# Linear attention and a gated feed-forward layer: attention steps at new places, ten sums of h in another layer

## The chip, the cores and the metric

The kernel runs on one core of a Trainium2 chip. The metric is the device time of one execution in microseconds (us); for the kernel before, the median of 11 executions is given. The core has a matmul engine (PE), a vector engine (DVE), a scalar engine (ACT), a general engine (POOL), and a queue that here only sends transfers (SP). Each works through its own instructions in order and waits for the others by semaphores.

## The reference

```python
# q, k, v: (8 batches, 8 heads, 576 positions, 64); all float32
kv  = einsum('bhsd,bhse->bhde', k, v)
out = einsum('bhsd,bhde->bhse', q, kv)
out = out / sqrt(mean(out * out, axis=-1) + 1e-6) * g_norm
x   = out.transpose(0, 2, 1, 3).reshape(4608, 512)
gate = 1 / (1 + exp(-(x @ w_gate)))       # w_gate, w_val: (512, 1536)
return (gate * (x @ w_val)) @ w_out       # w_out: (1536, 512)
```

The feed-forward weights come as 64-bit floats and are converted on the chip.

## The kernel before

**Chunks.** The 4608 rows of x are cut into nine chunks c = 0 to 8 of 512 rows; a batch of attention has 576 rows. Chunk 0 is computed plainly, while the first two batches of attention run and the weights are converted. From c = 1 on the first layer (`first_layer_fast`), and from c = 2 on the second layer too (`second_layer_fast`), use a scheme of fast matrix multiplication: a 4 x 4 by 4 x 2 block product (the second layer: the same with its own order) is done in 26 products of sums of blocks in place of 32. `PRODUCTS1` and `PRODUCTS2` list, for each product, the letter of the PSUM region that it adds into, the two forms that it multiplies (a form is a raw block, 0 to 15, or a sum from `SUMS`), and the steps that follow it: `o5=A` is a copy by ACT, `o3=o3+D` an add by DVE, `s0` a sigmoid by ACT, and `o5*o1` a multiplication by POOL (in the last product of the last third, by DVE). There are five PSUM regions for these letters, so a letter's region is taken, added into again, and given back.

**First layer.** It has three thirds j = 0, 1, 2 of 26 products each; the product i of third j stands at place p = 26 j + i, so places run from 0 to 77. A product is two matmuls of 128x256 in float32, which the profile records as four. After each product the program issues, in this order: the product's own steps (`combine`), the attention steps that a table has for this place (`at`), one sum of h (two at i = 12 and 25), and POOL's transfers.

**Attention.** While chunk c is computed, batch c + 1 of attention runs between its products (c = 1 to 6). `feed(b)` returns its steps. `kv_mm` multiplies k and v of all heads (80 matmuls), and `kv_copies` takes the result out in four steps on ACT. The heads come in four pairs n0 to n0 + 3. A pair's q has a single buffer: `turn` transposes it on DVE in two steps (t0 to t3 are the steps of the four pairs), and after the second step SP is told to load the next pair's q. `two_pairs` then works on two pairs at once (u0, u1), in nine steps: u_mm (144 small matmuls), square (ACT), two sums (DVE), root (ACT), two norms (DVE), and two x turns. An x turn is two transposes on DVE and twelve or fewer transfers that put x into the chunk that it belongs to. The k and v of the next batch are loaded by `load_late` at the end of each second layer, twelve transfers on SP's queue, into the space of `h_more`.

**Sums of h.** The first layer's result h of a third is the input of the second layer, which needs 28 sums of its blocks per third (`SUMS`). The sums of third j are issued by POOL during third j + 1; those of the last third in the second layer, eight of them by DVE (`ON_VECTOR`) and twenty by POOL, two ahead of the first product and two after each finished product (`finish`).

**Sums of x and w.** The sums of the next chunk's x (`X_SUMS`, 18 on DVE) are issued in the second layer after the finished products that `at2` names. The sums of the first layer's weights (`w1_sums`) are made once, by POOL, in chunk 0, written to memory and loaded back in parts ("granules", four per third) for each chunk. The sums of the second layer's weights pass through a ring of ten buffers: ten loads (`load_w`) stand in the first layer and eight in the second, all on POOL's queue.

Of the kernel before, what the change touches and what calls it, by code (L numbers as in the profile page):

```python
# [20 lines left out]
def kernel(  # L21
# [13 lines left out]
    B, H, S, HD = q.shape  # L35
# [43 lines left out]
    first = first_ctx.__enter__()  # L79
# [274 lines left out]
    def feed(b):  # L354
# [94 lines left out]
        def turns_of(n):  # L449
# [3 lines left out]
        kv = [kv_mm] + [lambda i=i: kv_copies(i, range(3)) for i in range(2 * NC)]  # L453
        t0, t1, t2, t3 = (turns_of(n0 + i) for i in range(4))
        u0, u1 = two_pairs(n0), two_pairs(n0 + 2)
        return kv, list(zip(
            (3, 4, 19, 20, 28, 30, 31, 33, 34, 35, 36, 39, 41, 42, 45, 46, 48, 51, 53, 55, 56, 57, 61, 64, 71, 72),
            t0 + t1 + u0[:2] + t2[:1] + u0[2:3] + t2[1:] + u0[3:7] + t3 + u0[7:] + u1))

    def flush():  # L460
        while fill:
# [249 lines left out]
        s_ = h_at[v]  # L711
        return h_main[j][:, s_] if s_ < 4 * NT else h_more[:, j, s_ - 4 * NT]

    def h_sums(j):
        ops = []
        for v, (x, sign, y) in SUMS.items():
            eng = nc.vector if j == N3 - 1 and v in ON_VECTOR else nc.gpsimd
            ops.append((eng, lambda v=v, x=x, sign=sign, y=y, eng=eng: eng.tensor_tensor(  # L718
                out=h_form(v, j), in0=h_form(x, j), in1=h_form(y, j), op=op_of(sign))))
        return ops  # L720
# [12 lines left out]
    def w1_sums(j):  # L733
        for v in W_ORDER:
            x, sign, y = SUMS[v]
            nc.gpsimd.tensor_tensor(out=w1_slot(j, w_at[v]), in0=w1_slot(j, w_at[x]), in1=w1_slot(j, w_at[y]),  # L736
                                    op=op_of(sign))
# [43 lines left out]
    for f in range(4, NFT):  # L781
        if f == NFT - 1:
            last = at_ps()
            plain(0, f, (last[:, 0], last[:, 1]))
        else:
            plain(0, f, (mm_ps(), mm_ps()))
        if f == 8:
            second_batch[0][0]()
        elif f == 9:
            for step in second_batch[0][1:]:  # L790
                step()
        elif f == NFT - 1:
            w1_sums(0)
            w1_sums(1)

    ps = [mm_ps() for _ in range(G // P)]
# [106 lines left out]
    def first_layer_fast(c, at):  # L903
        for f in range(NFT):
            gv_tile(c, f)
        for j in range(N3):
            o = {f"t{n}": pair(temps[:, i]) for i, n in enumerate((0, 1, 8, 9))}
            for n in (3, 1, 2, 0):
                o[f"o{n}"] = pair(sg_tile())
            h = h_main[j].rearrange("p (g e t) c -> p g e (t c)", g=2, e=2)  # L910
            for n in range(4):
                o[f"o{4 + n}"] = h[:, :, n // 2, GH * (n % 2):GH * (n % 2) + GH]
            regions = {}
            for i, (name, hv, wv, steps) in enumerate(PRODUCTS1):
                part, p = next(n for n, r in enumerate(PARTS) if i in r), NPR * j + i
                new = name not in regions
                if new:
                    i_ = free.popleft()
                    regions[name] = i_, pair(bank(i_))
                ws = w1_form(c, j, part, hv)  # L920
                for g in range(2):
                    nc.tensor.matmul(regions[name][1][:, g], ws[:, g], xf[c][wv], start=(new and g == 0), stop=True,  # L922
                                     skip_group_check=True)
                combine(o, regions, steps, nc.vector if j == N3 - 1 and i == NPR - 1 else nc.gpsimd)
                give_all(regions, LAST1, i)
                for step in at.get(p, ()):
                    step()
                for _ in range(2 if i % HALF == HALF - 1 else 1):
                    if h_fill:
                        h_fill.popleft()[1]()  # L930
                if c > 1:
                    g_ = NPA * (N3 * (c - 2) + j) + part
                    if i == PARTS[part][-1] and p < NPR * N3 - 1:
                        load_granule(g_ + NPA)
                    k_, r = divmod(p - 30, 4)
                    if r == 0 and 0 <= k_ < NR:
                        load_w((c - 2) * NS + k_)
                elif p in (NPR, 2 * NPR):
                    keep_w1(j - 1)
                elif p == 2 * NPR + HALF:  # L940
                    for g_ in range(NPA):
                        load_granule(g_)
            if c > 1:
                h_fill.extend(h_sums(j))

    tok = [slice(P * i, P * i + P) for i in range(NT)]

# [63 lines left out]
    def second_layer_fast(c, at):  # L1011
        o = {f"t{n}": temps[:, i, 0:DH] for i, n in enumerate((0, 1, 8, 9))}
        rows = [sg_tile() for _ in range(NT)]
        for t in range(NT):
            for n in range(2):
                o[f"o{2 * t + n}"] = rows[t][:, DH * n:DH * n + DH]
        regions, used, done = {}, {}, count()
        dones = {18: 0, 22: 1, 24: 2, 25: 3}

        def product(i, js):  # L1020
            name, hv, wv, _ = PRODUCTS2[i]
            if i not in used:
                used[i] = name not in regions
                if used[i]:
                    regions[name] = take()
            ws = w_raw(wv) if wv < 8 else ring((c - 2) * NS + STREAM.index(wv))
            for j in js:
                nc.tensor.matmul(regions[name][1], h_form(hv, j), ws[:, j], start=(used[i] and j == 0),  # L1028
                                 stop=(j == N3 - 1), skip_group_check=True)

        def finish(i):
            _, _, wv, steps = PRODUCTS2[i]
            combine(o, regions, steps, nc.gpsimd)
            give_all(regions, LAST2, i)
            if wv > 7 and STREAM.index(wv) + NR < NS:
                load_w((c - 2) * NS + STREAM.index(wv) + NR)
            if i == 16:
                load_granule(NPA * N3 * (c - 1) + NPA - 1)
            if i in dones:
                t = dones[i]  # L1040
                if c == NG - 1 and t == NT - 1:
                    store(c, t, rows[t], slice(0, DH), (nc.sync, nc.scalar))
                else:
                    store(c, t, rows[t])
            elif c == NG - 1 and i == 23:
                store(c, NT - 1, rows[NT - 1], slice(DH, DM))
            for step in at.get(next(done), ()):
                step()
            sums_of_h(2)

        on_pool = deque(step for eng, step in h_fill if eng is nc.gpsimd)

        def sums_of_h(n):
            for _ in range(n):
                if on_pool:
                    on_pool.popleft()()

        sums_of_h(2)
        for eng, step in h_fill:
            if eng is nc.vector:  # L1060
                step()
        h_fill.clear()
        blocks, some = range(N3), range(N3 - 1)
        product(0, blocks)
        finish(0)
        for i in (1, 2, 6):
            product(i, some)
        product(3, blocks)
        finish(3)
        for i in range(1, NPR):  # L1070
            if i != 3:
                if i in (1, 2, 6):
                    if i == 6:
                        continue
                    product(i, (N3 - 1,))
                    finish(i)
                    if i == 2:
                        product(6, (N3 - 1,))
                        finish(6)
                else:  # L1080
                    product(i, blocks)
                    finish(i)
        load_late(c + 2)
# [11 lines left out]
    for c in range(1, NG):  # L1095
        at1, at2 = {}, {}
        if c + 1 < B:
            kv, first_ = second_batch if c == 1 else feed(c + 1)
            for p, step in first_ + ([(16 + p, step) for p, step in enumerate(kv)] if c > 1 else []):
                at1.setdefault(p, []).append(step)  # L1100
        if c + 1 < NG:
            p0, two = (23, 18) if c == 1 else (6, 0)
            p = p0
            for n, step in enumerate(lambda n=n, c=c: x_sum(c + 1, n) for n in range(len(X_SUMS))):
                at2.setdefault(p, []).append(step)
                p += (2 if c == 1 else 1) if n % 2 or n >= two else 0
        if c == 1:
            for n, step in enumerate(w_forms()):
                at2.setdefault(2 * n, []).append(step)
        first_layer_fast(c, at1)  # L1110
        if c == 1:
            sgs += [spare_sg] + more_sgs
        (second_layer_plain if c == 1 else second_layer_fast)(c, at2)
# [30 lines left out]
```

## Time and profile before

| What | us |
|---|---|
| median of 11 executions | 1050.69 |
| lowest and highest | 1046.60 and 1056.12 |
| the profiled execution | 1047.59 |
| its span in the profile | 1045.8 |
| PE busy | 1019.8 |
| DVE busy | 721.1 |
| POOL busy | 607.4 |
| ACT busy | 348.3 |

The profiled execution is one of the lower ones; its span leaves out 1.8 us around it. From the timeline of PE, the starts of the layers (us):

| c | first layer starts | lasts | second layer starts | lasts |
|---|---|---|---|---|
| 1 | 161.88 | 75.44 | 237.32 (plain) | 41.20 |
| 2 | 278.52 | 76.06 | 354.58 | 34.03 |
| 3 | 388.62 | 76.30 | 464.92 | 33.80 |
| 4 | 498.72 | 76.35 | 575.07 | 33.79 |
| 5 | 608.85 | 77.46 | 686.32 | 34.43 |
| 6 | 720.74 | 78.83 | 799.57 | 33.76 |
| 7 | 833.33 | 67.34 | 900.67 | 36.50 |
| 8 | 937.18 | 67.38 | 1004.56 | 41.25, with the end |

Lines of the profile are read so: in a list of waits, who waited for whom, then us in total, how often, and the longest. In a timeline: start, us, engine, line of the program, operation, out<-in, shape and count, and in brackets the idle time of the engine just before and what ended it. In the chain of waits: start, us, what. In a table of stretches: the stretch, its length, then the busy time and count of PE, PEld, DVE, ACT and POOL, the clock, the share of the DMA engines, and GB/s.

### The profile page before, as it was taken

What the parts mean: (1) busy time and instruction counts of PE and PEld (TensorE: products, weight loads), DVE (VectorE), ACT (ScalarE), POOL (GpSimd) and SP (SyncE); (2) the same over time, 40 slices, a digit from 0 to 9 for tenths busy, and PEclk for the clock granted to TensorE, in tenths of its full rate; (3) what the DMA queues carried; (4) which work ended last, traced back from release to release, by engine and by line L of the source; (5) the groups of instructions that cost most, each with busy time, mean ns of one, the idle gap of its engine ahead of it and who ended that gap; (6) DMA issues with size and microseconds to landing.
All of it is one profiled execution on the core that took longest, in us unless ns stands there. A gap on an engine that the chain in (4) does not pass through costs nothing.

```text
span 1045.8 us, 18194 instructions
## 1 busy us (share of the span) xinstructions
PE 1019.8 (98%) x6854; PEld 814.1 (78%) x6854; DVE 721.1 (69%) x1188; ACT 348.3 (33%) x604; POOL 607.4 (58%) x991
## 2 busy tenths in 40 slices
PE   9999999999999999999999999999999999999998
PEld 8544447784588888888888888788788888788876
DVE  4899898676557955776577756785488556755672
ACT  4653423440144204431444125411442033213320
POOL 0002999876148832985179507790488239923991
PEclk9999999999999999999999999999999999999999
DMA  9975301469768656865777576766576536653634
GB/s 265 262 250 178 119 27 52 154 222 354 253 183 252 215 168 217 259 219 167 226 232 244 173 208 198 228 194 177 172 253 210 164 109 231 209 159 113 233 112 116
DMA packets 98406, 203.31 MB, mean 194 GB/s; under 512 B 29840, under 2 KB 69008, under 8 KB 98320
## 3 DMA queue, kind: packets, MB, share of 16 engines
q0 software_dynamic: 28048, 138.43, 39.7%
q1 hardware_dynamic: 70016, 63.66, 21.8%
q8 instruction: 54, 0.88, 0.4%
q14 instruction: 32, 0.26, 0.1%
q10 hardware_dynamic: 256, 0.07, 0.0%
HBM read 168.30 MB, written 26.74 MB: 186 GB/s over the span
## 4 chain that ended last, share of the span: by engine, by line
PE 74%; POOL 12%; DVE 5%; DMA 4%; issue 2%; ACT 2%; SPq 0%; POOLq 0%; DVEq 0%; ACTq 0%
PE mm L922 32%; PE mm L1028 21%; PE mm L559 7%; PE mm L1001 4%; PE mm L799 4%; POOL h L718 4%; POOL h_more L718 3%; POOL h L885 3%; DMA q<-in_q_dram 3%; PE at L407 2%; DVE sg L893 1%; DVE h L893 1%; POOL w L967 1%; PE at L366 1%; DMA h_more<-in_v_dram 1%
## 5 line engine op out<-in xcount | busy, mean ns | idle before, releaser
L922 PE MATMUL mm<-xs,w 128*128 128x256 f32 x1428 | 335.0, 380 | 5.3 <-DVE sg L893 5.3
L922 PEld LDWEIGHTS mm<-xs,w 128*128 128x128 f32 x1428 | 269.5, 190 | 45.8 <-DVE sg L893 8.8
L922 PE MATMUL mm<-xT,w 128*128 128x256 f32 x948 | 231.4, 380 | 4.2 <-ACT temps L889 4.2
L922 PEld LDWEIGHTS mm<-xT,w 128*128 128x128 f32 x948 | 179.0, 190 | 32.3 <-ACT temps L889 5.3
L893 DVE TENSOR_TENSOR sg<-sg,mm 128x512 f32<-128x512 f32 (+1 forms) x169 | 99.0, 604 | 147.5 <-PE mm L922 100.5
L762 POOL DMA_DIRECT2D w<-kept x84 | 46.4, 552 | 228.1 <-PE mm L922 227.7
L1028 PE MATMUL mm<-w,h 128*128 128x256 f32 x558 | 127.2, 379 | 0.6 <-POOL h L885 0.5
L889 ACT COPY temps<-mm 128x512 f32<-128x512 f32 (+1 forms) x124 | 64.3, 540 | 182.7 <-PE mm L922 99.4
L885 POOL TENSOR_TENSOR h<-h,sg 128x512 f32<-128x512 f32 x72 | 93.8, 1321 | 46.8 <-ACT sg L882 26.8
L1028 PEld LDWEIGHTS mm<-w,h 128*128 128x128 f32 x558 | 105.9, 190 | 15.7 <-POOL h L885 1.4
L718 POOL TENSOR_TENSOR h<-h 128x128 f32<-128x128 f32 x189 | 99.1, 535 | 9.5 <-DVE h_more L718 6.4
L882 ACT ACTIVATE sg<-sg 128x512 f32<-128x512 f32 x96 | 59.0, 629 | 114.7 <-DVE sg L893 114.4
L1028 PE MATMUL mm<-w,h_more 128*128 128x256 f32 x390 | 90.4, 381 | 3.9 <-POOL h_more L718 3.8
L889 ACT COPY sg<-mm 128x512 f32<-128x512 f32 (+1 forms) x107 | 55.3, 516 | 93.3 <-PE mm L1028 47.4
L1028 PEld LDWEIGHTS mm<-w,h_more 128*128 128x128 f32 x390 | 73.4, 190 | 16.1 <-POOL h_more L718 5.0
L559 PE MATMUL mm<-xT,w 128*128 128x512 f32 x176 | 77.7, 594 | 0.0
L893 DVE TENSOR_TENSOR temps<-temps,mm 128x512 f32<-128x512 f32 (+1 forms) x93 | 58.1, 624 | 19.5 <-PE mm L1028 10.8
L736 POOL TENSOR_TENSOR h_more<-w 128x256 f32<-128x256 f32 x10 | 12.9, 1302 | 97.0 <-PE at L366 97.0
L889 ACT COPY h<-mm 128x512 f32<-128x512 f32 x48 | 28.1, 585 | 119.7 <-PE mm L922 119.7
L893 DVE TENSOR_TENSOR temps<-mm,temps 128x512 f32<-128x512 f32 (+1 forms) x62 | 39.0, 628 | 38.4 <-PE mm L922 16.3
L967 POOL DMA_DIRECT2D w<-kept x102 | 63.1, 619 | 2.4 <-issue 2.2
L559 PEld LDWEIGHTS mm<-xT,w 128*128 128x128 f32 x176 | 32.6, 190 | 37.0 <-issue 36.4
(144 smaller groups left out, 1414.1 us busy)
## 6 DMA issues: line engine op xcount, KB each, us to landing
w<-kept POOLq DMA_DIRECT2D x102, 384.0 KB, 4.2
w<-kept POOLq DMA_DIRECT2D x42, 896.0 KB, 5.9
w<-kept POOLq DMA_DIRECT2D x42, 768.0 KB, 5.8
w_ring<-kept POOLq DMA_DIRECT2D x24, 384.0 KB, 4.0
out_dram<-sg SPq DMA_DIRECT2D x110, 64.0 KB, 1.7
q<-in_q_dram SPq DMA_DIRECT2D x24, 288.0 KB, 6.4
st<-in_moe_w_gate_dram SPq DMA_DIRECT2D x12, 512.0 KB, 5.6
st<-in_moe_w_val_dram SPq DMA_DIRECT2D x12, 512.0 KB, 6.3
```

Of the source, the lines that this page charges most:

```text
L559: nc.tensor.matmul(self.ps[i], w[("wg", "wv")[i], self.f][:, m, :], xT[self.c][:, m, :], start=(m == 0), stop=(m == NMT - 1), skip_group_c ...
L718: ops.append((eng, lambda v=v, x=x, sign=sign, y=y, eng=eng: eng.tensor_tensor(out=h_form(v, j), in0=h_form(x, j), in1=h_form(y, j), op=op ...
L762: nc.gpsimd.dma_start(out=granule(g)[:, 0:n], in_=kept1[g // NPA % N3, g % NPA][:, 0:n])
L799: nc.tensor.matmul(ps[t], gv[0, f][:, P * t:P * t + P], w["wo", f], start=(f == 0), stop=(f == NFT - 1), skip_group_check=True)
L882: nc.scalar.activation(out=o["o" + step[1]], in_=o["o" + step[1]], func=AF.Sigmoid)
L885: mult.tensor_tensor(out=o[x], in0=o[x], in1=o[y], op=ALU.mult)
L889: nc.scalar.copy(out=o[out_], in_=o[expr])
L893: tt(out=o[out_], in0=o[x], in1=o[y], op=ALU.add if sign == "+" else ALU.subtract)
L922: nc.tensor.matmul(regions[name][1][:, g], ws[:, g], xf[c][wv], start=(new and g == 0), stop=True, skip_group_check=True)
L967: nc.gpsimd.dma_start(out=ring(i), in_=kept3[i % NS].rearrange("p (j n) -> p j n", j=N3))
L1001: nc.tensor.matmul(ps, gv[c, f][:, tok[t]], w2[:, f, :], start=(n == 0), stop=(n == NFT - 1), skip_group_check=True)
L1028: nc.tensor.matmul(regions[name][1], h_form(hv, j), ws[:, j], start=(used[i] and j == 0), stop=(j == N3 - 1), skip_group_check=True)
```

## The change

Four things are changed.

1. `feed` places its steps anew, and leaves the last two (the two x turns of u1) to the second layer: after finishes 4 and 5, or, in the plain second layer of c = 1, after matmuls 4 and 8. The steps of kv_mm and kv_copies go from places 16 to 20 to 17, 17, 19, 20 and 22. The sums of x in the second layer then begin after finish 12 in place of 6, the first eight of them two at a time (not in c = 1, nor where no attention is left).
2. Of the 28 sums of h of third j = 1, only 18 are issued in third j = 2; the ten others are issued in the second layer, behind the first 18 of j = 2 and ahead of that third's last ten.
3. The ten loads of the ring stand at places 20, 22, ... 38 in place of 30, 34, ... 66.
4. `w1_sums(0)` is issued after the plain block f = 10 in place of f = 15.

The places of the attention steps, c = 1 to 6:

| Step | before | after |
|---|---|---|
| turns of pair n0 | 3, 4 | 1, 5 |
| turns of n0 + 1 | 19, 20 | 14, 22 |
| u0: u_mm, square | 28, 30 | 27, 30 |
| turns of n0 + 2 | 31, 34 | 29, 31 |
| u0: sums, root | 33, 35, 36 | 32, 33, 37 |
| turns of n0 + 3 | 42, 45 | 38, 47 |
| u0: norms, x turns | 39, 41, 46, 48 | 46, 49, 52, 53 |
| u1: u_mm, square, sums, root | 51, 53, 55, 56, 57 | 53, 55, 56, 57, 60 |
| u1: norms | 61, 64 | 61, 63 |
| u1: x turns | 71, 72 | second layer, finishes 4 and 5 |

```diff
-        return kv, list(zip(
-            (3, 4, 19, 20, 28, 30, 31, 33, 34, 35, 36, 39, 41, 42, 45, 46, 48, 51, 53, 55, 56, 57, 61, 64, 71, 72),
-            t0 + t1 + u0[:2] + t2[:1] + u0[2:3] + t2[1:] + u0[3:7] + t3 + u0[7:] + u1))
+        first = list(zip((1, 5, 14, 22, 27, 29, 30, 31, 32, 33, 37, 38, 46, 47, 49, 52, 53, 53, 55, 56, 57, 60, 61, 63),
+                         t0 + t1 + u0[:1] + t2[:1] + u0[1:2] + t2[1:] + u0[2:5] + t3[:1] + u0[5:6] + t3[1:] + u0[6:] +
+                         u1[:7]))
+        return kv, first, u1[7:]
...
-    def h_sums(j):
+    SUMS_FIRST = 18
+
+    def h_sums(j, some):
         ops = []
-        for v, (x, sign, y) in SUMS.items():
+        for v, (x, sign, y) in list(SUMS.items())[some]:
...
+        elif f == 10:
+            w1_sums(0)
         elif f == NFT - 1:
-            w1_sums(0)
             w1_sums(1)
...
-                    k_, r = divmod(p - 30, 4)
+                    k_, r = divmod(p - 20, 2)
                     if r == 0 and 0 <= k_ < NR:
                         load_w((c - 2) * NS + k_)
...
-                h_fill.extend(h_sums(j))
+                h_fill.extend(h_sums(j, slice(SUMS_FIRST) if j else slice(None)))
...
+        for j in (1, 2):
+            h_fill.extend(h_sums(j, slice(SUMS_FIRST, None)))
         on_pool = deque(step for eng, step in h_fill if eng is nc.gpsimd)
...
-            kv, first_ = second_batch if c == 1 else feed(c + 1)
-            for p, step in first_ + ([(16 + p, step) for p, step in enumerate(kv)] if c > 1 else []):
+            kv, first_, then = second_batch if c == 1 else feed(c + 1)
+            for p, step in (list(zip((17, 17, 19, 20, 22), kv)) if c > 1 else []) + first_:
                 at1.setdefault(p, []).append(step)
+            for p, step in zip((4, 8) if c == 1 else (4, 5), then):
+                at2.setdefault(p, []).append(step)
         if c + 1 < NG:
-            p0, two = (23, 18) if c == 1 else (6, 0)
+            p0, two = (23, 18) if c == 1 else (12, 8) if c + 1 < B else (6, 0)
```

## The prediction

> **What bounds the kernel now.** I read the page first, then the waits of the matmul engine (PE), then its timeline and the chain of waits inside one chunk, and last the queues that the moved steps pass through (DVE, ACT, POOL, SP).
>
> ```profile
> span 1045.8 us, 18194 instructions
> PE 1019.8 (98%) x6854; PEld 814.1 (78%) x6854; DVE 721.1 (69%) x1188; ACT 348.3 (33%) x604; POOL 607.4 (58%) x991
> ...
> PE mm L922 <- DVE sg L893: 5.9, 7, 1.6
> PE mm L922 <- ACT temps L889: 4.2, 6, 0.8
> PE mm L1028 <- POOL h_more L718: 3.8, 3, 1.8
> PE at L372 <- DMA h_more<-in_v_dram: 2.4, 1, 2.4
> PE mm L922 <- ACT sg L889: 1.8, 1, 1.8
> ```
>
> PE is the bound: 98% busy at the full clock. Only its idle moments can be won, and PE's waits (us, times, longest) name them. All seven on DVE and all six on ACT lie in the first layers with attention, c = 1 to 6. The timeline of PE in c = 3, a typical chunk, shows two:
>
> ```profile
> 435.48 1.03 PE L922 MATMUL mm<-xs,w 128*128 128x256 f32 x4
> 437.50 1.13 PE L922 MATMUL mm<-xs,w 128*128 128x256 f32 x4 [1.00 <-DVE sg L893]
> ...
> 443.93 4.48 PE L922 MATMUL mm<-xs,w 128*128 128x256 f32 x20
> 449.08 1.13 PE L922 MATMUL mm<-xT,w 128*128 128x256 f32 x4 [0.67 <-ACT temps L889]
> ```
>
> A product is four matmul records in 0.867 us (20 records start within 4.33 us). After 435.48 the next should start at 436.35; it starts at 437.50 and needs 0.97 instead of 0.867. So a stall costs its bracketed gap plus 0.26 us (the modelled end hides 0.16, the restart 0.1). The chain of waits in the same stretch says why:
>
> ```profile
> 425.25 7.26 DMA q<-in_q_dram
> 432.51 0.02 issue
> 432.53 0.57 DVE qTs L383
> ...
> 446.46 1.28 ACT L419
> 447.74 0.01 issue
> 447.76 0.31 ACT ms L419
> 448.07 0.97 ACT temps L889 x2
> ```
>
> First stall (A): DVE has turns of q, sums and norms between the adds of products i = 6 to 18, is busy from 422 to 441 us, and is late with o3=o3+D of i = 21, which product i = 24 must await before it adds into D again. Second stall (B): the root at place 57 (i = 5) puts a table load of 1.28 and the root of 0.31 ahead of t9=E and t8=C of i = 7, and product i = 8 adds into C.
>
> Chunks 7 and 8 have no attention; there POOL is late:
>
> ```profile
> 856.00:905.00 49.00, 48.46 (x225) 42.35 (x224) 33.81 (x48) 15.28 (x27) 46.77 (x79) 1.00 0.65 220
> ...
> 908.15 0.70 PE L1028 MATMUL mm<-w,h_more 128*128 128x256 f32 x2 [1.76 <-POOL h_more L718]
> ```
>
> In the first line (a stretch of c = 7) POOL, the fifth pair, is busy for 46.77 of 49.00 us: it arrives behind at the first sums of third j = 2, which product 3 of the second layer reads.
>
> [...] the copies at 448.07 stand behind the root. [...] the trace shows the 1.28, and 0.01 of issue after it, so I use 1.28 alone. [...]
>
> **The change part by part.**
>
> *New places in j = 1 and 2.* Stall B: the second root goes to place 60 (i = 8), after t8=C. Next in ACT's queue is t0=F (i = 9), which product 13 overwrites: four products, 3.5 us, against 1.6 for the root. B is gone. Stall A: the steps are now at i = 1 to 7 (no adds before 6), root i = 11, a turn i = 12, then nothing until norm 0 at i = 20 (0.26 + 0.7), a turn at 21 and norm 1 at 23. For c = 3: the two turns at 29 and 31 run as soon as u_mm and the q load let them, about place 29.6; the q load sent then needs 7.3 us (that of 425.25 took 7.26) and lands at about place 38, where the next turn stands. DVE then has eight adds of 0.6 us, 4.8, for products 13 to 18 (5.2 us), and o3=o3+D ends about 0.9 us before product 24 wants it. A is gone with 0.9 us to spare. Also gone: in c = 5 the stall at 684.48 (0.39), where x turns stood at 71 and 72.
> Gaps that go: c = 1: 0.56 + 0.83; c = 2: 0.72 + 0.67; c = 3: 1.00 + 0.67; c = 4: 0.80 + 0.67; c = 5: 1.61 + 0.67 + 0.39; c = 6: 0.79 + 0.67. Sum 10.05 over 13 stalls, plus 13 x 0.26 = 3.4: **13.4 us**. The stall of 1.78 in c = 1 stays: ACT there waits for a buffer that POOL releases after w1_sums(2), at 193.7 whatever happens.
>
> *kv_mm one place later (17).* In c = 6 it waited 2.38 + 0.18 for the k and v transfer; one product covers 0.87 of that: **0.9 us**. Elsewhere it is only swapped with a product. The last kv copy now comes at place 22 and u_mm at 27: estimated end of the copy 0.2 to 0.7 us ahead of u_mm in c = 3. I take 0; 0.3 in each chunk if ACT slips.
>
> *The turn of the second q pair, place 19 to 14: the added wait.* Its load stands in SP's queue behind the stores and the 12 transfers of load_late, which the change doesn't move. In c = 3 it is sent at 399.73 and takes 6.8 us, to 406.5: 17.9 us after the chunk's start. In c = 2, 4, 5, 6: 16.9, 19.0, 17.7, 20.2. Place 14 is reached after 13.0 us. So DVE stands 4 to 7 us at this turn, and behind it o7=t1-E (i = 15), o1=G-o1 and the adds of 17 and 18. PE doesn't feel it at once: products 15 to 18 need nothing from them (F is free, G and D wait for ACT), and kv_mm (2.5 us) lies between. Product 19 adds into E after o7; it is due at 19.0 us (18 products more and kv_mm), 21.0 in c = 6. o7 is done 1.3 us after the landing (turn 0.5, add 0.7, signal 0.1). Stalls: c = 2 none, c = 3 0.25, c = 4 1.3, c = 5 0, c = 6 0.5; with 0.15 each for restarts **2.4 us lost**. In c = 1 no load_late stands ahead and the load takes 3 us: none.
>
> *Ten sums of j = 1 to the second layer, ring loads from place 20 in steps of 2.* In c = 7, POOL loses 10 x 0.46 and three ring loads of 0.56 (six loads stood in j = 1 and four in j = 2; now three stand in j = 0, where POOL idled, and seven in j = 1): 6.3 us less where it was 1.8 behind. Stalls of c = 7 (0.54 + 1.76), c = 8 (1.75) and c = 5 (0.27): 4.32 + 4 x 0.26 = **5.4 us won**. In the second layer POOL has 16.84 of 33 us filled; 4.6 more fit. The first moved form, 41, is needed at product 18, 23 us in; at two sums per finish it is issued by the ninth, 12 us in. In j = 1 POOL has 7 loads in place of 6, denser; granules come up to 2.4 us later, against 17 us until use.
>
> *x turns in the second layer, x sums from finish 12.* The turns (4 x 0.38 us on DVE) run 8 to 9.6 us in; their 12 transfers take 0.64 each in SP's queue, the last lands near 18; the first sum stands at 16.9. DVE waits about 1 us there and has, for 18 sums of 0.34 and 17 adds, 12 to 13 us of work in 16.9. Cost 0, up to 0.3 per chunk. Stores come later in SP's queue.
>
> *w1_sums(0) at f = 10.* POOL waits for kv_mm (f = 8) until 98.33 and then works without a break; nothing else stands in its queue between. 0.
>
> **Sum.** 13.4 + 0.9 + 5.4 - 2.4 = 17.3 us. The profiled execution took 1047.59 (span 1045.8 and 1.8 around), 3.1 below the median of 1050.69. Taken from the median: 1033.4; I say 1034.
>
> **Rivals.**
> 1. *Ring loads crowd the q loads.* From 412 to 435 us of c = 3, ten loads of 384 KB and five granules are asked for, some 8 MB, where the record shows up to 349 GB/s. For it: the load of 425.25 took 7.26 with ring loads about, that of 409.22 only 5.7. Against: [...] 7.26 was already such a case. At 10 us, A comes back nearly whole, 1.2 in five chunks: 6 less, 1040.
> 2. *The stalls only move*, for DVE's work is the same: then the POOL part and kv remain, 6.3: 1044. Against: DVE idles 4.75 us at a stretch elsewhere in each third.
> 3. *Slower: the turn at place 14.* All five chunks stall by landing + 1.3 - 19.0. Without the 2.4, the rest gains 19.7; it is used up at 3.9 us per chunk, a landing at 21.6. At 23 us: 5 x 5.3 = 26.5, 1057. For it: nothing is moved ahead of this load, c = 6 shows 20.2, and executions up to 1056 suggest later transfers. Against: four of five land before 19.1.
>
> **How the numbers follow.** Forecast 0.6 (1027 to 1039), rival 1 0.12, rival 2 0.13, rival 3 0.1; 0.05 for more than forecast or an unseen offset. The floor is the gross gain of 19.7 and some hidden restarts: 1027. The top, 1046, takes in rivals 1 and 2. This measurement can't tell less than 0.3%, 3.2 us, from no change. Faster 0.85, same 0.05 (half-way cases of 2 and 3), slower 0.1.
>
> **What would show it.** No PE wait on ACT temps and none of 0.8 us or more on DVE sg at i = 24; a new PE wait on DVE h (o7) right after kv_mm, largest in c = 4; attention first layers near 74 to 75.5 us instead of 76.1 to 78.8; no POOL wait at product 3 in c = 7 and 8. The forecast is wrong if the q load behind load_late lands after 21 us, if q loads take 9 us or more, or if PE waits for u_mm's kvq.

## The result and the profile after

The kernel after takes 1038.85 us (median of 13 executions, 1036.50 to 1047.01); before, measured again beside it, 1051.07 (49 executions). The ratio is 0.9897, interval 0.9875 to 0.9919: 12.2 us less, where 17.3 were forecast (1034, range 1027 to 1046).

The profiled execution took 1042.19, 3.3 above its median, while the one of before lay 3.1 below its own. So the two profiles differ by 5.7 us of span only, and have to be compared wait by wait. Two lines of the page of the kernel after:

```profile
span 1040.1 us, 18190 instructions
...
PE 1019.4 (98%) x6854; PEld 817.6 (79%) x6854; DVE 719.6 (69%) x1188; ACT 347.9 (33%) x604; POOL 604.8 (58%) x991
```

PE is still the bound, with the same busy time; the idle moments fell. Its waits in the kernel after (us in total, times, longest):

```profile
PE mm L1032 <- DVE sg L897: 3.4, 4, 1.4
PE mm L926 <- ACT sg L893: 2.6, 1, 2.6
PE mm L926 <- DVE h L897: 2.5, 3, 1.6
PE at L407 <- issue: 2.1, 1, 2.1
PE at L372 <- DMA h_more<-in_v_dram: 1.7, 1, 1.7
```

The old waits on DVE sg and ACT temps in the first layers are gone from the list, and so is that on POOL at the second layer. (L926 is the first layer's matmul, formerly L922; L1032 the second layer's, formerly L1028.) In their place stand three new kinds: on DVE in the second layers, on DVE h behind kv_mm, and "issue" (nothing that the profile shows) in c = 4. The wait on ACT in c = 1 and that for k and v were there before. From the starts of the layers on PE's timeline, in us:

| c | first layer, before | after | second layer, before | after |
|---|---|---|---|---|
| 1 | 75.44 | 75.76 | 41.20 | 41.20 |
| 2 | 76.06 | 76.11 | 34.03 | 36.17 |
| 3 | 76.30 | 75.10 | 33.80 | 34.97 |
| 4 | 76.35 | 78.40 | 33.79 | 34.47 |
| 5 | 77.46 | 73.85 | 34.43 | 34.42 |
| 6 | 78.83 | 76.37 | 33.76 | 34.05 |
| 7 | 67.34 | 67.34 | 36.50 | 33.67 |
| 8 | 67.38 | 67.34 | 41.25 | 38.92 |

A layer without a stall is seen in c = 5 (73.85) and c = 7 (67.34 and 33.67). The stretch in which c = 3 formerly stood twice, on PE's timeline of the kernel after:

```profile
437.22 1.03 PE L926 MATMUL mm<-xs,w 128*128 128x256 f32 x4
438.08 1.03 PE L926 MATMUL mm<-xT,w 128*128 128x256 f32 x4
438.94 2.11 PE L926 MATMUL mm<-xs,w 128*128 128x256 f32 x8
440.89 1.89 PE L926 MATMUL mm<-xT,w 128*128 128x256 f32 x8
442.62 1.03 PE L926 MATMUL mm<-xs,w 128*128 128x256 f32 x4
443.57 1.80 PE L407 MATMUL at<-kvq,qTs 32*64 32x64 f32 x144
445.30 1.13 PE L926 MATMUL mm<-xT,w 128*128 128x256 f32 x4
446.27 4.60 PE L926 MATMUL mm<-xs,w 128*128 128x256 f32 x20
450.71 1.03 PE L926 MATMUL mm<-xT,w 128*128 128x256 f32 x4
```

No bracket is left. Product 24 of j = 1 is in the line at 438.94: eight records in 1.95 us, which is 0.2 more than 1.73, and the only trace of stall A.

**The turn at place 14.** DVE's timeline in c = 2 of the kernel after, and then PE's:

```profile
298.41 0.57 DVE L383 STREAM_TRANSPOSE qTs<-q 96x384 f32<-96x384 f32 x1 [5.09 <-DMA q<-in_q_dram]
```

```profile
296.91 1.13 PE L926 MATMUL mm<-xs,w 128*128 128x256 f32 x4
299.62 1.13 PE L926 MATMUL mm<-xs,w 128*128 128x256 f32 x4 [1.58 <-DVE h L897]
```

DVE stands 5.09 us for the load and takes its adds in order: the first of them behind the turn starts at 298.92. PE stands 1.58 behind kv_mm. The load landed 19.5 us after the chunk's start; 19.5 + 1.33 - 19.0 = 1.8, and the stall is 1.58 + 0.26.

**The sums of x.** The first sum of x in the second layer of c = 2 on DVE's timeline, and PE's timeline behind it:

```profile
372.81 0.42 DVE L897 TENSOR_TENSOR sg<-temps 128x256 f32<-128x256 f32 x1
376.40 1.08 DVE L825 TENSOR_TENSOR xs<-xT 128x256 f32<-128x256 f32 x2 [3.17 <-DMA xT<-xTs]
```

```profile
379.06 1.56 PE L1032 MATMUL mm<-w,h 128*128 128x256 f32 x6 [0.61 <-DVE temps L897]
381.98 2.21 PE L1032 MATMUL mm<-w,h 128*128 128x256 f32 x9 [1.36 <-DVE sg L897]
```

The transfers of the x turns that this sum needs have landed 21.2 us after the layer's start, not near 18; DVE waits 3.17 us, the adds behind it are late, and PE pays 0.61 + 1.36 and two restarts. The list of transfers in the profile of before shows how long such a transfer takes (how many, KB each, median us from issue to landing):

```profile
xT<-xTs SPq DMA_DIRECT2D x48, 72.0 KB, 3.8
```

**The pause in c = 1 and the clock.** PE's wait on ACT there grew from 1.78 to 2.56 us. In a table of stretches (PE's busy time and count first, the granted clock third from the right):

```profile
190.00:195.00 5.00, 2.54 (x12) 1.90 (x10) 0.00 (x0) 1.76 (x4) 5.00 (x5) 1.00 0.11 40
...
196.00:199.00 3.00, 3.00 (x8) 2.38 (x8) 2.20 (x4) 0.02 (x1) 3.00 (x7) 0.51 0.69 266
199.00:202.00 3.00, 3.00 (x15) 2.64 (x15) 1.55 (x3) 2.18 (x3) 3.00 (x7) 1.00 0.84 296
```

Behind the pause PE ran for 3.4 us at half its clock: 8 matmul records in 3 us against 15 in the next 3. That costs another 1.7 us. The same follows a pause of 2.12 in u_mm of c = 4, which the profile puts down to "issue": from 557.36 to 560.77 the granted clock is 0.50. This makes the first layer of c = 4 the slowest after.

### The profile page after: what moved, and what is told of

It reads as the page before. It is cut to its first block, busy times and chain, and to the rows that moved or that the text cites. A ratio compares the mean times of both kernels' runs of the same rounds, so it can differ in the third digit from the quotient of the medians.

```text
span 1040.1 us, 18190 instructions
## 1 busy us (share of the span) xinstructions
PE 1019.4 (98%) x6854; PEld 817.6 (79%) x6854; DVE 719.6 (69%) x1188; ACT 347.9 (33%) x604; POOL 604.8 (58%) x991
## 4 chain that ended last, share of the span: by engine, by line
PE 55%; DMA 4%; DVE 3%; SPq 2%; issue 1%; DVEq 0%
PE mm L926 37%; PE mm L1032 16%; DMA xT<-xTs 2%; DMA q<-in_q_dram 2%; DVE xs L825 1%; PE at L407 1%; SPq L442 1%; DVE sg L897 1%; DMA h_more<-in_k_dram 1%; DVE xs L827 1%; PE at L366 0%; DVE temps L897 0%; SPq L502 0%; SPq L123 0%; DVE h L897 0%
## 5 line engine op out<-in xcount | busy, mean ns | idle before, releaser
L926 PE MATMUL mm<-xs,w 128*128 128x256 f32 x1428 | 334.8, 381 | 2.6 <-DVE h L897 2.5
L926 PEld LDWEIGHTS mm<-xs,w 128*128 128x128 f32 x1428 | 271.1, 191 | 42.4 <-DVE h L897 3.8
L926 PE MATMUL mm<-xT,w 128*128 128x256 f32 x948 | 231.8, 382 | 0.0
L926 PEld LDWEIGHTS mm<-xT,w 128*128 128x128 f32 x948 | 180.0, 191 | 25.9 <-issue 1.0
L1032 PE MATMUL mm<-w,h 128*128 128x256 f32 x558 | 127.6, 380 | 3.6 <-DVE sg L897 2.9
L1032 PEld LDWEIGHTS mm<-w,h 128*128 128x128 f32 x558 | 105.6, 190 | 19.8 <-DVE sg L897 4.6
L1032 PE MATMUL mm<-w,h_more 128*128 128x256 f32 x390 | 88.9, 379 | 0.0
L1032 PEld LDWEIGHTS mm<-w,h_more 128*128 128x128 f32 x390 | 74.1, 190 | 10.1
L721 POOL TENSOR_TENSOR h_more<-h 128x128 f32<-128x128 f32 x105 | 51.5, 493 | 30.6 <-DVE h L889 27.2
```

## The experiments

Eleven more kernels ran, and the kernel after once more, each timed against the kernel before on the same chip; ratios are to that.

Half clock lengthens an execution without any wait, and differs between executions: the mean granted clock of those of before in these series runs from 0.992 to 1.000. Its share can be estimated, for this mean is on record for every execution: time x clock is roughly what the execution would have taken at full clock (PE is busy for 98% of the span). This is called the clock-free time below; with clocks of three decimals and five or six executions it is good to 1 or 2 us. The kernel after has a median of 1036.8 clock-free, 1036.9 when it ran again; before has 1048.8, 1048.7, 1048.6 and 1047.5 in the four series of the experiments. On average half clock took 3.1 us in the kernel after and 2.8 to 3.6 in the four series of before.

**Sums of x later** (e1_xsums_16)

```diff
-            p0, two = (23, 18) if c == 1 else (12, 8) if c + 1 < B else (6, 0)
+            p0, two = (23, 18) if c == 1 else (16, 18) if c + 1 < B else (6, 0)
```

> The kernel after, with the sums of the next chunk's x from finish 16 on, two at a time, in place of finish 12. Theory (the x turns' transfers land 4 to 5 us after they are sent, DVE stands at the first sum of x, and PE pays): the PE waits on DVE at finishes 13 to 15 of the second layers of c = 2 to 6 go, second layers of 33.7 to 33.9 us in place of 36.2, 35.0, 34.5, 34.4 and 34.1, the time about 4 to 5 us below the kernel after, near 1034. Rival (the wait hides behind PE, the seconds are lost elsewhere): no change from 1038.9. Second rival: the late sums run into the next first layer, whose products 16 to 23 want them; PE waits there and half or more is given back.

1038.46 us, ratio 0.9866 (0.9832 to 0.9900). In the profile the mechanism is confirmed: the second layer of c = 2 (36.17 in the kernel after) and those of c = 3 to 6 have lost their stalls (a table of stretches, c = 2, 3 and 4):

```profile
355.68:389.35 33.67, 33.67 (x158) 29.64 (x157) 22.97 (x57) 3.35 (x9) 19.18 (x39) 1.00 0.53 152
468.35:502.02 33.67, 33.67 (x157) 29.64 (x156) 23.20 (x57) 3.35 (x9) 18.94 (x39) 1.00 0.52 151
577.84:611.51 33.67, 33.67 (x157) 29.64 (x156) 22.66 (x57) 3.36 (x9) 19.46 (x39) 1.00 0.51 151
```

But the median fell by 0.4 us only, within what six executions can tell. Clock-free it is 1033.8, 3.0 below the kernel after; half clock took 4.7 us on average in place of 3.1. PE's timeline in the first layer of c = 3 of this execution shows where some of it went:

```profile
409.41 0.69 PE L366 MATMUL at<-h_more 128*64 128x64 f32 x16 [2.81 <-DMA h_more<-in_v_dram]
410.03 0.46 PE L372 MATMUL at<-h_more 64*64 64x64 f32 x16
410.42 3.42 PE L926 MATMUL mm<-xs,w 128*128 128x256 f32 x8
```

PE waits 2.81 us for v, and the eight records behind it need 3.2 us in place of 1.73, at half the clock (0.50 from 411 to 414). By its number the first rival (no change) came out, but not by its cause: the stalls of the second layers were on PE's path and are gone, and the gain is hidden by more half clock and by the waits for k and v. The second rival falls: the next first layers don't wait for sums of x.

**The turn back at 19** (e2_turn_19)

```diff
-        first = list(zip((1, 5, 14, 22, 27, ...
+        first = list(zip((1, 5, 19, 22, 27, ...
```

> The kernel after, with the first turn of the second q pair at place 19 in place of 14. Theory (DVE stands at this turn until a load behind load_late has landed, and PE at product 19 waits for landing + 1.3 - 19.0 us): the PE waits on DVE h right after kv_mm go (1.6, 0.6 and 0.3 us in c = 2, 3 and 6), 2 to 3 us below the kernel after, near 1036. Rival (the turn, now behind, delays the turn at 22, the next load of q and with it the turns at 29 to 38, so the stall that the change took away comes back): no gain, or 1 to 4 us slower than the kernel after, with PE waits on DVE sg at product 24 of j = 1.

1034.72 us, ratio 0.9824 (0.9795 to 0.9853): about 4 us below the kernel after (also clock-free: 1032.7), more than the 2 to 3 expected. No wait on DVE h is left in PE's list of waits:

```profile
PE mm L1032 <- DVE sg L897: 3.5, 4, 1.3
PE mm L926 <- ACT sg L893: 1.8, 1, 1.8
PE at L372 <- DMA h_more<-in_v_dram: 1.5, 1, 1.5
```

The rival falls: no wait at product 24 came back. A second gain is in the line on ACT: the pause in c = 1 is 1.8 again. In the six profiles with the turn at 14 and POOL's multiplications kept (the kernel after twice, and experiments 1, 3, 5 and 11) it is 2.3 to 2.6, in this one and the four with the old places 1.8.

**Both POOL parts undone, or done alone** (e3_pool_undone, e4_pool_alone, e8_sums_alone, e9_ring_alone)

```diff
# e3, from the kernel after:
-                h_fill.extend(h_sums(j, slice(SUMS_FIRST) if j else slice(None)))
+                h_fill.extend(h_sums(j, slice(None)))
-        for j in (1, 2):
-            h_fill.extend(h_sums(j, slice(SUMS_FIRST, None)))
-                    k_, r = divmod(p - 20, 2)
+                    k_, r = divmod(p - 30, 4)
# e4, from the kernel before: the reverse of these edits
# e8, from the kernel before: the sums alone;  e9: the ring loads alone
```

> The kernel after, with the 28 sums of h of j = 1 back in third j = 2 and the ring loads back at places 30, 34, ... 66. Theory (POOL was behind by 1.8 us at the second layer of c = 7 and 8): these two stalls come back, 36.2 to 36.5 us for these second layers in place of 33.7, and about 5 us are lost against the kernel after, near 1044; more, up to 8, if POOL is behind in c = 2 to 6 as well, now that PE is faster there. Rival (the new places alone suffice, POOL's stall was a matter of this profile): within 1 us of the kernel after.

> The kernel before, with the ten sums of j = 1 moved to the second layer and the ring loads at 20, 22, ... 38, and nothing else. Theory: 5.4 us below the kernel before, near 1045.5, with the second layers of c = 7 and 8 at 33.7 and the stalls in the first layers as before. Rival (ring loads crowd the q loads in SP's queue): q loads of c = 2 to 6 in j = 1 take 9 us or more, PE's wait at product 24 grows by 1 to 2 us per chunk, and the time is that of before or slower.

> The kernel before, with only the ten sums of j = 1 moved to the second layer. Theory (the sums relieve POOL, the early ring loads cost the q loads): the waits on POOL in c = 7 and 8 go, PE's wait at product 24 of j = 1 stays at 0.7 to 1.6 us, about 5 us below the kernel before, near 1046. Rival (the sums themselves slow DVE or POOL in the second layer, or give nothing without the ring loads moved too): within 2 us of the kernel before.

> The kernel before, with only the ring loads moved to places 20, 22, ... 38. Theory: PE's wait at product 24 of j = 1 grows from about 1 to 2.3 us, as it did with both parts moved, with a fall of the clock behind some of these pauses, while the waits on POOL in c = 7 and 8 shrink by 1.7 us or stay: 2 to 6 us slower than the kernel before. Rival (the wait grew by chance of that execution): within 2 us of the kernel before, wait at product 24 near 1 us.

| Kernel | median us | ratio | interval |
|---|---|---|---|
| e3, from after: both undone | 1044.37 | 0.9935 | 0.9916 to 0.9954 |
| e8, from before: sums alone | 1046.87 | 0.9941 | 0.9919 to 0.9963 |
| e9, from before: ring loads alone | 1057.87 | 1.0057 | 1.0034 to 1.0081 |
| e4, from before: both alone | 1054.50 | 1.0018 | 0.9995 to 1.0041 |

The sums alone bring what was forecast for the POOL part: 5.3 us, with the second layer of c = 7 at 33.67. The ring loads alone cost 5.7, and both together bring nothing: rival 1 of the prediction, at the old places. The waits of PE with the ring loads alone, and then the chain of waits in its c = 4 (start, us, what):

```profile
PE mm L922 <- DVE sg L893: 12.7, 6, 2.7
PE mm L922 <- ACT temps L889: 4.2, 6, 0.8
```

```profile
545.91 8.51 DMA q<-in_q_dram
554.42 0.02 issue
554.44 0.57 DVE qTs L383
...
559.37 0.04 issue
559.41 2.93 PE mm L922 x6
```

The q load takes 8.51 us in place of 7.0 in the same chunk of before; DVE is later by that much, and PE's waits on DVE sg, nearly all at product 24, grow from 5.9 us in total to 12.7. Behind five pauses (four of these and one for v) the clock fell to half: 0.57 on average from 446 to 450, behind one of them, and 0.991 over the execution. By the estimate most of the price is that: clock-free the ring loads alone take 1049.1, only 0.4 more than before (the waits on POOL fell by 2.7 us in this profile, and the profile of before is one of the lower ones), while half clock took 8.1 us on average in place of 3.0. With both parts it is 1047.0, 1.8 less than before, and 7.3 in place of 3.2. In the kernel after, the q loads sent at places 22 and 31 took 2.9 to 6.4 us, and this wait isn't there.

With the parts undone from the kernel after, the waits on POOL are back (6.8 us in four second layers, c = 2, 5, 7 and 8), and the loss of 5.5 us in the medians is as expected.

**Multiplications of c = 1, j = 0 on DVE** (e6_mult_dve)

```diff
-                combine(o, regions, steps, nc.vector if j == N3 - 1 and i == NPR - 1 else nc.gpsimd)
+                combine(o, regions, steps, nc.vector if (j == N3 - 1 and i == NPR - 1) or (c == 1 and j == 0) else nc.gpsimd)
```

> The kernel after, with the four multiplications of third j = 0 of c = 1 done by DVE in place of POOL, so that ACT's copy at i = 5 of j = 1 doesn't wait for POOL to end the sums of the weights. Theory (PE's pause there, 1.8 to 2.6 us, costs itself and, when the clock falls to half for 3.4 us behind it, 1.7 us more): the pause in c = 1 goes, first layer of c = 1 near 71.5 us in place of 73.5 to 75.8, 2 to 4 us below the kernel after, 1035 to 1037. Rival (the pause is only put off, POOL's later work holds ACT or DVE instead): within 1 us of the kernel after.

1037.41 us, ratio 0.9866 (0.9836 to 0.9895). ACT no longer waits for POOL; PE's pause of 2.56 has become one of 0.78 on DVE, without a fall of the clock (the eight records from 184.35 on take their usual 1.89), and the first layer of c = 1 takes 72.26 in place of 75.76:

```profile
183.41 1.10 PE L926 MATMUL mm<-xs,h_more 128*128 128x256 f32 x4 [0.78 <-DVE sg L897]
```

So the pause was POOL's lateness after the sums of the weights. In the time, 1.4 us between medians is less than these series can tell apart.

**Weights' sums back** (e5_w1_back)

```diff
-        elif f == 10:
-            w1_sums(0)
         elif f == NFT - 1:
+            w1_sums(0)
```

> The kernel after, with the sums of the weights of j = 0 issued after block f = 15 in place of f = 10. Theory (POOL waits for kv_mm until 98 us either way): POOL's first sum at 98 to 98.5 us and the last at 188.5 to 189.5, the time within 1 us of the kernel after. Rival (the earlier issue starts POOL sooner, or is behind the longer pause of c = 1): POOL's sums end 1 us or more elsewhere, and the first layer of c = 1 moves with them.

1043.32 us over six executions, ratio 0.9911 (0.9882 to 0.9940), which overlaps the kernel after. POOL's first sum starts at 98.94 (98.36 after, 98.33 before), 0.6 us late like the whole of that execution, and its pause in c = 1 is again 2.56. Its sums end at 190.11 (189.53 after), later by the same. The expected nothing is what the trace shows; the time, 4.5 us above the kernel after where less than 1 was expected, doesn't confirm it.

**Ring loads back at the old places, all else as after** (e11_ring_late), and **the kernel after once more** (after_again)

```diff
-                    k_, r = divmod(p - 20, 2)
+                    k_, r = divmod(p - 30, 4)
```

> The kernel after, with only the ring loads back at places 30, 34, ... 66. Theory (the early loads cost q loads at the old places; at the new ones the q loads miss them, being 3 to 5 us long; POOL has 4.6 us of room by the sums alone): within 1.5 us of the kernel after, no wait on POOL in c = 7 and 8. Rival 1 (the early loads still hurt): 2 us or more below the kernel after. Rival 2 (the loads in j = 1 and 2 crowd the last q loads and POOL): 2 us or more above it, with waits at product 24 or on POOL.

> The kernel after, once more. The two last comparisons (ring loads late, weights' sums back) stand or fall with how far executions of the kernel after itself differ: its first series had 13 executions from 1036.5 to 1047.0. If the late ring loads really cost 6 us, this series has its median near 1039 again; if they cost little and the series differ by that much among themselves, it is at 1041 to 1045. In its profile, a pause of 1.8 to 2.6 us in the first layer of c = 1 in either case, and with the clock at half behind it where the pause is the longer.

Late ring loads: 1045.22, ratio 0.9934 (0.9911 to 0.9958). The kernel after again: 1039.42, ratio 0.9893 (0.9857 to 0.9929), so its series repeat. The theory (within 1.5 us) falls: at the new places the early ring loads seem to help, by about 4 us if the ratios are compared, whose intervals overlap. Clock-free the late loads take 1040.0; but e5, timed beside them, takes 1040.2, also some 3 us above the kernel after, without an edit that its trace shows to cost anything. So part of the 4 may belong to the series and not to the loads. The cause stays open: the profile of the late loads is that of its lowest of 22 executions (1037.16) and shows no wait on POOL and none at product 24. Nor do the parts add up: with both POOL parts undone the time is the same as with the ring loads alone undone, though only the former's profile has waits on POOL.

**Edits together** (e7_all, e10_kv_later): e7 has the edits of e1, e2 and e6; e10 moves kv_mm as well:

```diff
-            for p, step in (list(zip((17, 17, 19, 20, 22), kv)) if c > 1 else []) + first_:
+            for p, step in (list(zip((19, 19, 21, 22, 24), kv)) if c > 1 else []) + first_:
-        first = list(zip((1, 5, 19, 22, 27, ...
+        first = list(zip((1, 5, 19, 22, 28, ...
```

> The kernel after, with three edits together: sums of x from finish 16, the first turn of the second q pair at place 19, and the multiplications of c = 1, j = 0 on DVE. Theory (the three costs add): about 5 us from the sums of x, 4 from the turn and 2 to 4 from c = 1, near 1028 to 1030, and what is left is PE's wait for k and v at kv_mm. Rival (one pays for the other, since PE that comes earlier meets later transfers): 1032 or more, with longer waits for k and v.

> The three edits together, and besides kv_mm and its copies at places 19, 19, 21, 22 and 24 in place of 17, 17, 19, 20 and 22, with the first u_mm at 28 in place of 27. Theory (what is left is PE's wait for k and v, 1.6 to 2.1 us in two or three chunks, at times with the clock at half behind it): two products cover 1.7 us of each, 2 to 4 us below the three edits alone, near 1030. Rival (the copies now end after u_mm, or the turn at 19 stands behind kv_mm): PE waits at u_mm instead, no gain or slower.

The three together: 1033.49, ratio 0.9820 (0.9794 to 0.9846), hardly below e2. The costs don't add; in its profile PE waits 2.0 and 2.1 us for k and v in c = 3 and 6. With kv_mm two products later: **1026.10 us** (1025.66 to 1029.08), ratio 0.9750 (0.9720 to 0.9781), below both kernels, and the four executions lie within 3.4 us where those of after spread over 10. All waits of PE from chunk 1 on in that profile:

```profile
PE at L407 <- issue: 1.0, 1, 1.0
PE mm L926 <- DVE sg L897: 0.9, 1, 0.9
...
PE at L372 <- DMA h_more<-in_v_dram: 0.3, 1, 0.3
```

No pause is over 1.1 us, and the clock doesn't fall before the end (its mean over the execution is 1.000). Two products are 1.7 us in each of at most five chunks; the gain of 7.4 over e7 is more than the waits of one profile. By the estimate the clock accounts for the rest: clock-free the median goes from 1030.4 to 1026.1, 4.3 less (PE's waits for k and v are 4.1 in the profile of e7 and 0.4 in this one), and half clock took 0.5 us on average in place of 2.9.

## Why the prediction was right, and where it was off

- **Stalls A and B, 13.4 us:** right. All thirteen are gone from the profile, but for 0.2 us at product 24. There was more room than forecast: the q load that was to need 7.3 us in c = 3 took 4.6.
- **POOL, 5.4 us:** right in size. The two profiles give 2.83 in c = 7 and 2.33 in c = 8, and the sums alone 5.3 in the time. The earlier ring loads did relieve POOL (alone they cut its stalls in c = 7 and 8 from 4.1 to 1.6 us), but their price on the q loads was put at nothing: alone at the old places they cost 5.7 us. That is rival 1, with a load of 8.5 us and not 10.
- **kv_mm, 0.9:** the wait of c = 6 went from 2.38 + 0.18 to 1.74, 0.8 less. That it would also show in c = 3 and limit further gains wasn't seen.
- **The turn at place 14, 2.4 lost** (its own terms add to 2.5)**:** the mechanism was right; measured 1.84, 0.90 and 0.59 in c = 2, 3 and 6, 3.3 in all. Landing + 1.33 - 19.0 (21.0 in c = 6) gives 1.8, 0.9 and 0.5; only the landings differ from those of before (19.5 in c = 2, 17.3 in c = 4). The wait was largest in c = 2, and c = 4, where it was to be largest, had none. Undone, it brought 4, for with it the pause of c = 1 is 0.8 longer too. This was rival 3's mechanism at a fifth of its price.
- **x turns and x sums, "Cost 0, up to 0.3 per chunk":** the step that failed. The second layers of c = 2 to 6 stand 2.5, 1.3, 0.8, 0.75 and 0.4 us above 33.67: 5.7 us. With the last transfer landing near 18, the forecast left it 1 to 2 us after it was sent. In c = 2 the twelve took 4.1 to 6.0 us from issue to landing, and the profile of before had 3.8 as the median of 48 like them. The 5.7 are one execution's price; e1, without it, gained 3.0 clock-free.
- **The pause of 1.78 in c = 1 "stays":** it grew to 2.56, with 1.7 us of half clock. Half clock after pauses was in no term. With the second fall and the "issue" pause of c = 4 it makes about 6.6 us of the profiled execution, of which 2.5 are in c = 1.
- **w1_sums(0) earlier, 0:** right, POOL's first sum starts at 98.36 in place of 98.33.

The terms of the profiled execution, 13.2 + 0.8 + 5.2 - 3.3 - 4.3 (the second layers of c = 2 to 6 together: 169.8 before, 174.1 after) - 2.5 - 4.1, give 5.0; the spans differ by 5.7. The median of the time gained 12.2, because the profiled execution after is among the slower ones of its kernel and that of before among the faster.

So the forecast's 17.3 was too high by 5. Half clock doesn't fill this gap in the medians, for it takes about as much from the kernel before as from the one after; the 3.4 us of it above belong to this pair of executions. By the clock-free times the waits for the x turns' transfers cost about 3 us, where nothing was counted, and the turn at 14 about 4, where 2.4 were: 4.7 more. That is an estimate, and it takes the two to add; with e6, which gained 2.0 clock-free, the three would bring 9.1 and brought 6.4.

## What to carry to other kernels

A step that waits for a transfer is placed by when that transfer lands in its own place in the queue, not by how long such transfers take elsewhere: count what stands ahead of it, and take the late landings (here 21.2 us into the layer, where 18 was forecast). The price was paid by the unrelated adds behind: DVE's 3.17 us at the first sum of x cost PE 0.61 and 1.36. A move that does no harm in company can be bad alone (the ring loads), so what covers each part should be named and tried. When many small stalls are removed, the one that remains takes over the gain: here PE then waited mainly for k and v, and two products of delay were worth more (7.4 us) than three other repairs (5.4), nearly half of it by half clock that no longer came.

## What the runs showed of the hardware

In the kernel after, PE's granted clock was 0.50 for 3.41 us at a time: from 195.55 on, behind the pause of 2.56, and from 557.36 on, behind the one of 2.12. Outside these two stretches it was 1.00 up to 1038.64. A pause of such a length was not always followed by this: the one of 2.38 in c = 6 of before was not, and there the clock stayed at 1.00 (736 to 746 us).

The two starts lie 361.81 us apart, which is 106 times 3.413; from the second to the fall after PE's last matmul, at 1038.64, it is 481.28, or 141 times. If the two profiles are laid out in such steps (that of before from its only fall, at 1042.75, behind its last matmul), the steps ahead of the four falls have 2.56, 2.12, 3.41 and 2.02 us in which PE is idle. No other step from c = 1 up to PE's last matmul has more than 1.76. The pause of 2.38 lies across two steps, with 0.97 in one and 1.41 in the next. That is a reading of two profiles and four falls; no run was made to test it.

The profile of the kernel after has PE pausing in c = 4 for 2.12 us on nothing that the profile shows, between the 139th and the 140th of the 144 small matmuls of a u_mm, which took 1.8 us in all where it didn't pause (443.57). In e10 it is 1.05 us between the same two. The lists of waits of e1, e2, e3, e6 and e11 have one such pause of 0.7 to 1.7 us at the same line, those of e4 and e8 one of 1.9 and 3.5 at the first layer's matmul; before and e9 have none. One queue of the page carries the name "instruction" and makes 54 transfers of 16 KB in the profile (packets, MB, share):

```profile
q8 instruction: 54, 0.88, 0.3%
```

The 31st of them was sent at 554.40 and landed at 555.47; the pause lasts from 554.73 to 556.85 and so ends 1.38 us after the landing. In before the 31st landed at 550.16, and PE came to the matmul of the same number at 552.06, 1.9 us later, without a pause. Whether PE waited for this transfer was not shown; no run tried to move it.

POOL's sums of the weights before c = 1 ended 0.7 us later in the kernel after, with the same sums in the same order (189.53 and 188.81), and PE's pause grew by as much. They took 90.9 to 91.2 us in the six profiles with the turn at 14 and POOL's multiplications kept, and 90.4 to 90.6 in the five with it at 19 or 20. Why is not known.
